# Group 0's x kept in SBUF: the heads' outputs copied straight into the split's input, the fourth heads moved by small DMAs, and the rows of w1 and w2 reordered to match

## The chip, the cores and the metric

One core of a Trainium2 chip runs the whole program. The metric is the time of one execution on the device in microseconds, as the median over several runs. PE is TensorE, DVE VectorE, ACT ScalarE, POOL GpSimd, SP SyncE; SP and POOL also issue DMAs.

## The reference

A gated linear attention, one token after the other, feeds a multiplicative feed-forward block. All inputs are float32 but the four weights, which arrive as 64-bit floats (the kernel reads them as pairs of 32-bit words and makes float32 of them itself).

```python
q, k, v, alpha: (4, 8, 768, 48)            # batch, heads, tokens, head size
for t in range(S):
    state = alpha[:, :, t, :, None] * state + einsum('bhd,bhe->bhde', k[:, :, t], v[:, :, t])
    y[:, :, t] = einsum('bhd,bhde->bhe', q[:, :, t], state)
x = y.transpose(0, 2, 1, 3).reshape(3072, 384)
a = x @ w1                                  # w1, w2: (384, 1024)
b = x @ w2
out = ((a * b) @ w3) @ w_out                # w3: (1024, 1024), w_out: (1024, 384)
```

## The kernel before

The 3072 tokens are 24 chunks of 128 (N), six to a batch entry; one turn n of the main loop, a step, handles one chunk. Three chunks make a group g of 384 tokens (TG), eight groups in all. Part 1 is the attention loop; while it runs, gate work for the groups 0 to 4 is mixed in. Part 2 does the rest of the gates, folds w3 with w_out into one matrix, and multiplies.

A step n of part 1 consists of: `load_a`, `load_kq`, `load_v` (loads for later steps, on SP); `scores(n)` (PE makes k times q into PSUM, VectorE masks it into `ms`, line 457); `transposed(n + 1)` (PE turns `qk` of the next chunk, line 381, ScalarE copies it to `qkT`, line 383); `attend(n - 1)` (PE, line 485, then ScalarE copies the heads' outputs to x, line 489); `outer(n)` (the state's update, lines 393 to 403); `decayed(n + 2)` (VectorE multiplies the loaded k and q by the decays, `qk`, line 359); `logs` and `decays` (the decays `e` of later chunks).

The weights' conversion stands between these: `load_gates` fetches 128 rows and 512 columns of w1 or w2 in one DMA (`raw`, line 236), ScalarE and VectorE make float32 of them (lines 244 to 253) and split it into a high part, a low part `l` (line 262) and a third part. The thirds of the first half are made by PE in `third` (lines 276, 277) and copied by ScalarE (line 278). Six of these conversions have to be done by the end of step 5.

x goes through DRAM: `attend` puts two stores per step into `later`, `store` issues them on SP (line 305) to `xd`, `load_x` brings a group back as `xT` with the model dimension on partitions (line 501), and `split_x` makes three parts of it (ScalarE line 507, VectorE lines 508 and 509). The row order of xT is that of the model dimension, so row p of part kk of the weights is row 128 kk + p of w1 or w2.

`gate` is a generator; `run(pieces)` advances it. A piece is nine matmuls of 128x128 by 128x384 (line 515), for one 128-column tile of w1 or w2: six for the first two parts, then three for the third. The group-0 split stands in step 6 (FIRST), `run(2)` in step 7 and further pieces by a table of step numbers:

```python
pieces = ((3, 3, 2, 0) if n > FIRST + 3 else (0, 3, 3, 0))[(n - FIRST) % 4] if n >= FIRST else 0
```

The order on each engine is not the program's order. A tile framework places the instructions on their engines by its own schedule and by the buffers' dependences; `after_marks` holds an instruction behind a named one in that schedule. Each engine then works through its list in order. SP's DMAs are told apart by eight DMA semaphores, taken in turn.

Of the kernel before, what the change touches and what calls it, by code (L numbers as in the profile page):

```python
# [48 lines left out]
def kernel(  # L49
# [29 lines left out]
    LATE = 10  # L79
    PAIRED = 8  # L80
    TURNED = 8
    assert D <= DP and DM % C == 0 and DF % CW == 0 and S % C == 0 and N % G == 0
    assert DM <= 512 and TG <= 512

# [138 lines left out]
    for x in Ts + decs:  # L223
        nc.gpsimd.memset(x, 0.0)

    def to_fp32(*srcs, width=None):

        n = width or sum(src.shape[1] for src in srcs)
        raw = rawp.tile([C, n], I64, tag="raw", name="raw")
        for i, src in enumerate(srcs):  # L230
            if width:
                rows = ds(i * src.shape[0], src.shape[0])
                to = raw[rows] if len(src.shape) == 2 else raw[rows].rearrange("p (b c) -> p b c", b=src.shape[1])
            else:
                to = raw[:, ds(i * src.shape[1], src.shape[1])]
            nc.sync.dma_start(out=to, in_=src)
        yield
        words = raw.bitcast(U32).rearrange("p (n w) -> p n w", w=2)
        low, high = words[:, :, 0], words[:, :, 1]

        mant = cvt.tile([C, n], FP32, tag="mant", name="mant")
        top = mant.bitcast(U32)
        rest = cvt.tile([C, n], FP32, tag="rest", name="rest", bufs=2)
        nc.scalar.activation(rest, low, AF.Copy, scale=2.0 ** -52)  # L244
        nc.vector.tensor_scalar(top, high, 0x000FFFFF, 0x00100000, op0=ALU.bitwise_and, op1=ALU.bitwise_or)

        power = cvt.tile([C, n], U32, tag="power", name="power", bufs=2)
        nc.vector.tensor_scalar(power, high, 20, 0x7FF, op0=ALU.logical_shift_right, op1=ALU.bitwise_and)  # L248
        nc.scalar.activation(power, power, AF.Relu, scale=2.0 ** 23, bias=rebias)  # L249
        yield  # L250
        nc.vector.scalar_tensor_tensor(mant, top, 2.0 ** -20, rest, op0=ALU.mult, op1=ALU.add)  # L251
        nc.vector.scalar_tensor_tensor(power, high, 0x80000000, power, op0=ALU.bitwise_and, op1=ALU.bitwise_or)  # L252
        nc.vector.tensor_mul(mant, mant, power.bitcast(FP32))  # L253
        yield
        return mant

    def load_gates(i, kk, half):
        w = yield from to_fp32((moe_w1, moe_w2)[i][ds(kk * C, C), ds(half * CW, CW)])
        h, l, m = (w12[half][:, x, i, kk, :] for x in range(3))
        nc.scalar.activation(h, w, AF.Copy, scale=(1.0 - 2.0 ** -13) / P)  # L260
        yield
        mark["l"] = nc.vector.scalar_tensor_tensor(l, h.bitcast(FP32), -P, w, op0=ALU.mult, op1=ALU.add).ins
        done.append((i, kk, half))
        if half:
            nc.vector.scalar_tensor_tensor(m, h.bitcast(FP32), P + 1.0, w, op0=ALU.mult, op1=ALU.subtract)
        else:
            thirds.append((m, h, l))
# [33 lines left out]
    def store():  # L301

        while later:
            dst, src = later.popleft()
            nc.sync.dma_start(out=dst, in_=src)
# [171 lines left out]
    def attend(n):  # L477
        (y, heads), ms, vc = st.pop(("y", n)), st.pop(("ms", n)), st.pop(("v", n))
        for j, i, to in heads:
            if turned(n):  # L480
                w = vts[n % 2][:, j, :] if i else vc[:, 2 * j, :]
                nc.tensor.matmul(to[:, DP:], w, ms[:, i, j, DP:], start=False,  # L482
                                 stop=(j % HP == HP - 1), skip_group_check=True)
            else:
                nc.tensor.matmul(to, vc[:, 2 * j + i, :], ms[:, i, j, :], start=(n % NCH == 0 and j % HP == 0),  # L485
                                 stop=(j % HP == HP - 1), skip_group_check=True)
        x = work.tile([C, HP, 2, C], FP32, tag="x", name="x", bufs=4)
        for i in range(2):
            copied = nc.scalar.copy(x[:, :, i], y[i])
        ends_of_part1[1] = copied.ins  # L490
        x = x.rearrange("p j i t -> p (j i) t")

        g, c = divmod(n, G)
        to = xd[g].rearrange("(b h d) t -> b d h t", b=2, d=D)
        for half in range(2):
            later.append((to[half, :, :, ds(c * C, C)], x[ds(DP * half, D)]))


    def load_x(g, queue=nc.sync):
        st["xT", g] = xp.tile([C, KM, TG], FP32, tag="xT", name="xT")  # L500
        queue.dma_start(out=st["xT", g], in_=xd[g].rearrange("(k p) t -> p k t", p=C))

    def split_x(g, i):
        x = st.pop(("xT", g))
# [79 lines left out]
    def gate(g, f):  # L584
        yield from (late_gate if late else early_gate)(g, f)
# [103 lines left out]
    for n in range(N + 1):  # L689
        if not 1 < n < FIRST:  # L690
            store()
        if n in loads:
            load_x(loads[n])
        if n != 1 and not 2 < n <= FIRST:
            load_a(n + 5)
        raws = (3, 3, 3, 3, 2, 2, 3, 3)[n] if n < 8 else 4
        for m in (n + 3,) * (n <= FIRST) + (n + 4,) * (n >= FIRST):
            load_kq(m)
            if 2 < n <= FIRST and m == n + 3:
                load_a(n + 5)  # L700
            if 1 < n < FIRST:
                store()
            if n < FIRST - 2:
                fetch(raws)
        if n >= FIRST:
            load_v(n + 2)
        if n:
            attend_state(n - 1)
        if n < N:
            scores(n)  # L710
        else:
            for j in range(NP):
                for i in range(2):
                    attend_low(n - 1, j % 2, i, i ^ (j < 2))
        transposed(n + 1)
        if n == 1:
            decays(3)
            load_a(6)
            with after_marks(("e", 3)):
                logs(4)  # L720
        if n == FIRST + 1:
            run(2)
        if n < FIRST:
            with after_marks("pool"):
                load_v(n + 2)
        if n - 2 in begin and n > FIRST:
            g, tiles = begin[n - 2]
            with after_marks(("ms", n), ("qkT", n + 1)):
                split_x(g, 0)
            fill.extend(gate(g, f) for f in tiles)  # L730
        if n == FIRST:
            with after_marks("l", ("qkT", n + 1)):
                split_x(0, 0)
            fill.extend(gate(0, f) for f in begin[n - 3][1])
        pieces = ((3, 3, 2, 0) if n > FIRST + 3 else (0, 3, 3, 0))[(n - FIRST) % 4] if n >= FIRST else 0
        if n == 0:
            with after_marks(("qkT", 0)):
                logs(2)
            decays(2)
            with after_marks(("e", 2)):  # L740
                logs(3)
        early, ready = n < FIRST, len(thirds) if n > 2 else n // 2
        marks = (*[("qkT", n + 1)] * (n < N - 1), *[("qk", n + 1), ("ms", n)] * early, *["x3"] * (n - 2 in begin and n > FIRST))
        if n < N - 2 and n != FIRST:
            with after_marks(*marks):
                convert(2 if early else 1, raws)
        advance(n)
        turn_v(n)
        if n:
            attend(n - 1)  # L750
        outer(n)
        if n > FIRST:
            third(ready)
        run(pieces > 0)
        if early:
            with after_marks(*marks):
                convert(1, raws)
        with after_marks(*[("ms", n)] * (n < 3)):
            decayed(n + 2)
        if not early:  # L760
            with after_marks(*[("qkT", n + 1)] * (n < N - 4)):
                logs(n + 4)
        if n == 4:
            load_x(0)
        convert(early and n > 0, raws)
        run(pieces > 1)
        if n:
            decays(n + 3)
        if n <= FIRST:
            third(ready)  # L770
        if 0 < n < FIRST:
            with after_marks(("e", n + 3)):
                logs(n + 4)
        if n == FIRST:
            with after_marks("x3", ("e", n + 3)):
                convert(2, raws)
        elif n < N - 2:
            convert(n == FIRST - 1 if early else n % 3 == 0, raws)
        if n == FIRST - 1:
            assert len(done) == 2 * KM  # L780
        run(pieces > 2)
        if n == N - 3:
            while begun:
                convert(1)
            weights.extend(load_out(j) for j in range(KF))
            fetch(4)
# [90 lines left out]
```

## Time and profile before

| what | value |
|---|---|
| time, median of 3 runs | 464.25 us (463.48, 464.25, 465.31) |
| span of the profiled execution | 462.8 us; its own total time isn't given beside it |
| busy share of PE, DVE, ACT, POOL | 97%, 80%, 60%, 21% |
| granted clock of TensorE | full in all 40 slices (digit 9) and 1.00 in the stretches |
| line 515, all gate matmuls on x and w | x1152, 337 ns each, 210.2 us |
| chain that ended last | PE 88%, DVE 4%, DMA 4%, ACT 2% |
| DMA packets | 148869, 80.37 MB; 97392 of them under 512 B |
| x stores on SP (`xd<-x`) | x48 of 96 KB, 3.9 us from issue to landing |
| x loads on SP and POOL (`xT<-xd`) | x5 and x9 of 576 KB, 5.0 and 4.7 us |
| weight loads on SP (`raw<-in_moe_w_dram`) | x12 of 512 KB, 5.8 us |

How to read it: a busy share is a mean over stages that have different limits. A chain of waits goes back from the last instruction and names at each point what released the next one. A busy PE has matmul ends that are modelled. Stretches are windows in microseconds from the span's start.

### The profile page before, as it was taken

What the parts mean: (1) busy time and instruction counts of PE and PEld (TensorE: products, weight loads), DVE (VectorE), ACT (ScalarE), POOL (GpSimd) and SP (SyncE); (2) the same over time, 40 slices, a digit from 0 to 9 for tenths busy, and PEclk for the clock granted to TensorE, in tenths of its full rate; (3) what the DMA queues carried; (4) which work ended last, traced back from release to release, by engine and by line L of the source; (5) the groups of instructions that cost most, each with busy time, mean ns of one, the idle gap of its engine ahead of it and who ended that gap; (6) DMA issues with size and microseconds to landing.
All of it is one profiled execution on the core that took longest, in us unless ns stands there. A gap on an engine that the chain in (4) does not pass through costs nothing.

```text
span 462.8 us, 11150 instructions
## 1 busy us (share of the span) xinstructions
PE 446.9 (97%) x4296; PEld 423.2 (91%) x4296; DVE 371.7 (80%) x610; ACT 276.4 (60%) x544; POOL 95.1 (21%) x186
## 2 busy tenths in 40 slices
PE   4998999999999999999999999999999999999996
PEld 2675699898999989999999999999999999999996
DVE  2779997999979988999998999997542967776671
ACT  4685975767658563988875676764545443333430
POOL 6234232325414430121221201212010000000000
PEclk9999999999999999999999999999999999999999
DMA  9999999999999974466856446412115875665511
GB/s 173 254 208 228 261 224 192 248 209 219 184 227 193 234 165 138 130 224 212 235 178 196 146 128 177 149 52 86 51 48 153 243 210 180 186 178 159 166 51 52
DMA packets 148869, 80.37 MB, mean 174 GB/s; under 512 B 97392, under 2 KB 138608, under 8 KB 148816
## 3 DMA queue, kind: packets, MB, share of 16 engines
q1 hardware_dynamic: 143040, 64.44, 57.3%
q0 software_dynamic: 5776, 15.22, 11.0%
q8 instruction: 34, 0.56, 0.5%
q14 instruction: 19, 0.16, 0.1%
HBM read 57.58 MB, written 22.06 MB: 172 GB/s over the span
## 4 chain that ended last, share of the span: by engine, by line
PE 88%; DVE 4%; DMA 4%; ACT 2%; issue 1%; SPq 0%; DVEq 0%; ACTq 0%
PE bank L515 72%; DMA kq<-in_q_dram 3%; PE bank L381 3%; PE bank L430 3%; PE bank L482 2%; PE bank L474 2%; PE bank L340 1%; PE bank L393 1%; PE bank L346 1%; PE bank L454 1%; PE bank L343 1%; PE bank L419 1%; DVE qk L359 1%; DVE ms L457 1%; PE bank L485 1%
## 5 line engine op out<-in xcount | busy, mean ns | idle before, releaser
L515 PE MATMUL bank<-x,w 128*128 128x384 f32 x1152 | 210.2, 337 | 1.7 <-ACT qkT L383 1.1
L515 PEld LDWEIGHTS bank<-x,w 128*128 128x128 f32 x1152 | 200.2, 188 | 4.1 <-ACT qkT L383 1.4
L515 PE MATMUL bank<-w3o,ab 128*128 128x384 f32 x576 | 100.2, 336 | 0.0
L515 PEld LDWEIGHTS bank<-w3o,ab 128*128 128x128 f32 x576 | 99.9, 188 | 0.0
L540 ACT ACTIVATE bank<-bank 128x384 f32<-128x384 f32 x96 | 45.6, 476 | 43.4 <-PE bank L515 43.1
L524 ACT ACTIVATE t<-bank 128x384 f32<-128x384 f32 x64 | 31.9, 499 | 54.9 <-PE bank L515 54.9
L590 POOL DMA_DIRECT2D abd<-ab x45 | 25.8, 573 | 137.9 <-DVE ab L576 121.3
L383 ACT COPY qkT<-bank 128x512 f32<-128x512 f32 x48 | 26.2, 596 | 24.8 <-PE bank L381 24.8
L641 DVE TENSOR_TENSOR ab<-abl,ab 128x1024 fp32r<-128x1024 f32 x24 | 29.3, 1223 | 12.3 <-ACT ab L640 12.3
L640 ACT ACTIVATE ab<-abl 128x1024 fp32r<-128x1024 f32 x24 | 25.5, 1061 | 20.2 <-PE bank L515 18.4
L515 PE MATMUL bank<-wo,w3T 128*128 128x384 f32 x192 | 35.9, 334 | 0.0
L576 DVE TENSOR_TENSOR ab<-bank,r 128x384 f32<-128x384 f32 x44 | 24.1, 548 | 12.5 <-PE bank L515 6.3
L515 PEld LDWEIGHTS bank<-wo,w3T 128*128 128x128 f32 x192 | 33.5, 188 | 0.0
L249 ACT ACTIVATE power<-power,rebias 128x512 uint32<-128x512 uint32 (+1 forms) x36 | 25.3, 701 | 12.6 <-DVE power L248 12.4
L359 DVE TENSOR_TENSOR qk<-kq,e 128x768 f32<-128x768 f32 x24 | 23.1, 964 | 11.3 <-ACT e L350 7.9
L526 DVE SCALAR_TENSOR_TENSOR o<-bank,t 128x384 f32<-128x384 f32 x24 | 13.4, 557 | 23.0 <-issue 13.7
L642 DVE SCALAR_TENSOR_TENSOR ab<-ab,abl 128x1024 fp32r<-128x1024 f32 x24 | 29.2, 1217 | 0.0
L526 DVE SCALAR_TENSOR_TENSOR r<-bank,t 128x384 f32<-128x384 f32 x40 | 22.0, 550 | 6.8 <-PE bank L515 3.4
L251 DVE SCALAR_TENSOR_TENSOR mant<-mant,rest 128x512 f32<-128x512 uint32 (+1 forms) x36 | 23.4, 649 | 3.7 <-ACT rest L244 3.7
L252 DVE SCALAR_TENSOR_TENSOR power<-raw,power 128x512 uint32<-128x512 uint32 (+1 forms) x36 | 23.5, 653 | 2.4 <-ACT power L249 2.4
L253 DVE TENSOR_TENSOR mant<-mant,power 128x512 f32<-128x512 f32 (+1 forms) x36 | 23.6, 655 | 0.5
L244 ACT ACTIVATE rest<-raw 128x512 f32<-128x512 uint32 (+1 forms) x36 | 23.3, 649 | 0.0
(102 smaller groups left out, 675.2 us busy)
## 6 DMA issues: line engine op xcount, KB each, us to landing
abl<-abd SPq DMA_DIRECT2D x24, 512.0 KB, 4.7
abd<-ab POOLq DMA_DIRECT2D x45, 192.0 KB, 3.2
raw<-in_moe_w_dram SPq DMA_DIRECT2D x64, 128.0 KB, 3.4
raw<-in_moe_w_dram SPq DMA_DIRECT2D x12, 512.0 KB, 5.8
xT<-xd POOLq DMA_DIRECT2D x9, 576.0 KB, 4.7
kq<-in_k_dram SPq DMA_DIRECT2D x24, 192.0 KB, 5.2
kq<-in_q_dram SPq DMA_DIRECT2D x24, 192.0 KB, 5.4
xd<-x SPq DMA_DIRECT2D x48, 96.0 KB, 3.9
```

The costliest lines, as they stand in the source:

```text
L249: nc.scalar.activation(power, power, AF.Relu, scale=2.0 ** 23, bias=rebias)
L359: mark["qk", n] = nc.vector.tensor_mul(qks[n % 3][:, :, :, 0:D], st.pop(("kq", n)), st.pop(("e", n)).rearrange("p i (h d) -> p i h d", h=H ...
L383: mark["qkT", n] = nc.scalar.copy(qkT[:, :, :, ds(DP * half, DP)], tp[half]).ins
L515: nc.tensor.matmul(p, w[part][i], x[part][i], start=start and part == parts[0] and i == 0, stop=stop and part == parts[-1] and i == n - 1, ...
L524: nc.scalar.activation(t, p1, AF.Copy, scale=(1.0 + 1.0 / P) * scale)
L526: nc.vector.scalar_tensor_tensor(to, p2, scale, t, op0=ALU.mult, op1=ALU.add)
L540: nc.scalar.activation(p, p, AF.Copy, scale=1.0 + 1.0 / P)
L576: nc.vector.tensor_mul(ab, p, r[0])
L590: (nc.gpsimd if late else nc.sync).dma_start(out=abd[g][:, f, :], in_=ab)
L640: nc.scalar.activation(t[:, 0], ab, AF.Copy, scale=1.0 - 2.0 ** -13)
L641: nc.vector.tensor_sub(t[:, 1], ab, t[:, 0].bitcast(FP32))
L642: nc.vector.scalar_tensor_tensor(t[:, 2], t[:, 0].bitcast(FP32), -1.0 - 1.0 / P, ab, op0=ALU.mult, op1=ALU.add)
```

## The change

For the chunks 0 to 2 (group 0), `attend` no longer stores x to DRAM. ScalarE copies the first three pairs of heads of each half from PSUM straight to their places in `xT`, and the fourth heads into a piece of `x`. Six DMAs per step, of 16 partitions by 128 columns each (8 KB), move those into partitions 48 to 63 and 112 to 127 of `xT`. So a row of xT is no longer a row of x in order: for part kk, partitions 0 to 47 hold head kk, the next 16 hold a third of head 3, and likewise for the second half. `load_gates` fetches the rows of w1 and w2 in that order, with four DMAs instead of one (48, 16, 48 and 16 rows), and `load_x` of the groups 1 to 7 fetches x with four DMAs as well. Group 0 is needed again in part 2: its xT is stored whole to `xd[0]` in step 7, and loaded with one DMA. The split of group 0 moves from step 6 to the end of step 5, its first two pieces of gates from the start of step 7 into step 6, and the thirds of step 6 ahead of them.

```diff
+    def runs(kk):
+        return [(i * DM // 2 + start, size, i * DP + at) for i in range(2)
+                for start, size, at in ((D * kk, D, 0), (D * KM + SD * kk, SD, D))]
...
     def load_gates(i, kk, half):
-        w = yield from to_fp32((moe_w1, moe_w2)[i][ds(kk * C, C), ds(half * CW, CW)])
+        src = (moe_w1, moe_w2)[i][:, ds(half * CW, CW)]
+        w = yield from to_fp32(*(src[ds(start, size)] for start, size, _ in runs(kk)), width=CW, at=[at for *_, at in runs(kk)])
...
         x = work.tile([C, HP, 2, C], FP32, tag="x", name="x", bufs=4)
+        if n < G:
+            if n == 0:
+                st["xT", 0] = xp.tile([C, KM, TG], FP32, tag="xT", name="xT")
+            to, part = st["xT", 0][:, :, ds(n * C, C)], x[:, HP - 1, 1]
+            nc.scalar.copy(part, y[1][:, HP - 1])
+            nc.scalar.copy(to[:, 0::2], y[0])
+            nc.scalar.copy(to[:, 1], y[1][:, 0])
+            for half in range(2):
+                for kk in range(KM):
+                    later.append((to[ds(half * DP + D, SD), kk], part[ds(half * DP + kk * SD, SD)]))
+            return
...
     def load_x(g, queue=nc.sync):
         st["xT", g] = xp.tile([C, KM, TG], FP32, tag="xT", name="xT")
-        queue.dma_start(out=st["xT", g], in_=xd[g].rearrange("(k p) t -> p k t", p=C))
+        if g == 0:
+            queue.dma_start(out=st["xT", g], in_=xd[g].rearrange("(p k) t -> p k t", k=KM))
+            return
+        for at in range(0, C, DP):
+            h = xd[g][ds(at // DP * DM // 2, DM // 2)]
+            queue.dma_start(out=st["xT", g][ds(at, D)], in_=h[0:KM * D].rearrange("(k p) t -> p k t", p=D))
+            queue.dma_start(out=st["xT", g][ds(at + D, SD)], in_=h[KM * D:].rearrange("(k p) t -> p k t", p=SD))
...
+        if n == FIRST + 1:
+            nc.sync.dma_start(out=xd[0].rearrange("(p k) t -> p k t", k=KM), in_=x0)
...
-        if n == FIRST + 1:
-            run(2)
...
-        if n == FIRST:
-            with after_marks("l", ("qkT", n + 1)):
-                split_x(0, 0)
-            fill.extend(gate(0, f) for f in begin[n - 3][1])
-        pieces = ((3, 3, 2, 0) if n > FIRST + 3 else (0, 3, 3, 0))[(n - FIRST) % 4] if n >= FIRST else 0
+        pieces = ((3, 3, 2, 0) if n > FIRST + 3 else (2, 3, 3, 0))[(n - FIRST) % 4] if n >= FIRST else 0
...
-        if n > FIRST:
+        if n >= FIRST:
             third(ready)
...
-        if n == 4:
-            load_x(0)
...
-        if n <= FIRST:
+        if n < FIRST:
             third(ready)
...
         if n == FIRST:
-            with after_marks("x3", ("e", n + 3)):
+            with after_marks(("e", n + 3)):
                 convert(2, raws)
...
         if n == FIRST - 1:
             assert len(done) == 2 * KM
+            x0 = st["xT", 0]
+            with after_marks("l"):
+                split_x(0, 0)
+            fill.extend(gate(0, f) for f in begin[FIRST - 3][1])
```

More of the change, by code (lines that the diff above doesn't have):

```diff
@@ L81 @@
     TURNED = 8
+    SD = D // KM
+    assert H == 2 * (KM + 1) and D % KM == 0 and D + SD == DP
     assert D <= DP and DM % C == 0 and DF % CW == 0 and S % C == 0 and N % G == 0
@@ L224, with to_fp32 @@
         nc.gpsimd.memset(x, 0.0)
-    def to_fp32(*srcs, width=None):
+    def runs(kk):
+        return [(i * DM // 2 + start, size, i * DP + at) for i in range(2)
+                for start, size, at in ((D * kk, D, 0), (D * KM + SD * kk, SD, D))]
+    def to_fp32(*srcs, width=None, at=None):
         n = width or sum(src.shape[1] for src in srcs)
@@ L231, in to_fp32 @@
             if width:
-                rows = ds(i * src.shape[0], src.shape[0])
+                rows = ds(at[i] if at else i * src.shape[0], src.shape[0])
                 to = raw[rows] if len(src.shape) == 2 else raw[rows].rearrange("p (b c) -> p b c", b=src.shape[1])
```

## The prediction

> **What bounds the kernel now.** I read the page's slices first, then busy time by stretches, the chain of waits, the waits of VectorE, the timeline of VectorE and ScalarE around the first split, and the DMA issues. After these I compared the order of instructions of the two kernels, engine by engine.
>
> The slices (40 of 11.6 us each) show three engines full at once in the first third:
>
> ```profile
> PE   4998999999999999999999999999999999999996
> DVE  2779997999979988999998999997542967776671
> DMA  9999999999999974466856446412115875665511
> ```
>
> The stretches say where TensorE still has idle time (columns: stretch, length, then busy us of PE, PEld, DVE, ACT, POOL, and the granted clock, DMA share and GB/s):
>
> ```profile
> 24.40:54.70 30.30, 27.41 (x409) 20.79 (x408) 26.15 (x44) 22.60 (x50) 10.17 (x17) 1.00 1.11 233
> 54.70:57.70 3.00, 3.00 (x38) 2.13 (x37) 2.71 (x5) 3.00 (x8) 0.83 (x2) 1.00 1.07 275
> 57.70:80.00 22.30, 22.30 (x318) 21.00 (x316) 19.76 (x38) 13.99 (x33) 7.14 (x15) 1.00 1.10 210
> 80.00:86.40 6.40, 5.30 (x125) 4.54 (x121) 5.63 (x9) 5.14 (x12) 2.31 (x3) 1.00 0.91 240
> ```
>
> From 54.7 us PE is full, with one hole of 1.1 us near 86, up to the end of part 1 (99.48 of 100.60 us busy from 86.4 to 187). So the end of the kernel is the moment at which PE becomes full, plus the work then left. Before 54.7 PE has 30.30 - 27.41 = 2.9 us of idle time, the most that an earlier start of gates can fill. The chain of waits shows who hands over to PE:
>
> ```profile
> 27.01 7.37 DMA kq<-in_q_dram
> 34.51 0.96 DVE qk L359
> ...
> 53.93 0.91 PE bank L343 x2
> ...
> 56.16 1.09 PE bank L454 x16
> 57.26 0.49 PE bank L381 x16
> 57.75 3.35 PE bank L515 x18
> ```
>
> VectorE leads, with one long wait for a load, until 50.4; then PE. Three pieces of attention work, 0.91 + 1.09 + 0.49 = 2.49 us (the decays of step 9, the scores of step 7, the transposes of step 8), stand on PE just ahead of the first 18 gate matmuls. Meanwhile VectorE and ScalarE make the split:
>
> ```profile
> 53.50 0.69 DVE L262 SCALAR_TENSOR_TENSOR w<-w,mant 128x512 fp32r<-128x512 f32 x1
> 54.11 1.28 DVE L457 TENSOR_TENSOR ms<-bank,keep 128x512 int32<-128x512 int32 x2
> 55.94 1.36 DVE L508 TENSOR_TENSOR x<-xT,x 128x1152 fp32r<-128x1152 f32 x1 [0.28 <-ACT x L507]
> 53.74 1.10 ACT L383 COPY qkT<-bank 128x512 f32<-128x512 f32 x2
> 54.68 1.22 ACT L507 ACTIVATE x<-xT 128x1152 fp32r<-128x1152 f32 x1
> ```
>
> The last weight part (L262) ends at 54.19 and the split starts on ScalarE at 54.68: x waited for neither its stores nor its load. xT had long landed, since L501 was issued at 49.08. So the trip through DRAM that the change takes away isn't what ends last here.
>
> **The change, part by part.** The profiled execution has a span of 462.8 us; the median of the runs is 464.25, 1.45 above. I work out a shift and add it to the median. A measurement of this kernel tells about 0.5% (2.3 us) from no change.
>
> *x of group 0 stays in SBUF.* Gone are six stores (0.44 us of SP each, median) and one load of 576 KB. New are 18 moves of 8 KB and, in step 7, a 576 KB store of xT. DMA work up to step 6 falls, by about 3 x 0.5 us for the stores (two that follow each other land 0.2 us apart) and about 2 us for the load. The path isn't there, so I take nothing; at best it shortens the waits for kq. The store in step 7 falls into DMA queues that are full (share 1.10), but qk finds its kq landed from 57.7 to 80, so: nothing. If that cover went, one such load (5.0 us to landing) would be its price.
>
> *ScalarE's copies.* Two copies of 256 columns (0.36 us each) become one of 256 and two of 128. From 384 columns at 0.48 and 256 at 0.36 a copy of 128 is about 0.24: +0.12 us in each of three steps, ScalarE being idle 25% of that stretch. Nothing; 0.4 us without the cover.
>
> *Weights.* Each of 12 loads of 512 KB becomes four (192, 64, 192, 64 KB), and xT loads of groups 1 to 7 four as well: SP gets 36 + 12 + 12 + 1 - 1 = 60 more issues, POOL 24 more. On POOL a load is issued right after the split before its own, a whole visit of gates ahead; one issue there is some 0.57 us (the row of `abd`), and PE is full: nothing, and 1.7 us per load without that cover. On SP, the order shows that each issue from the ninth on waits for one of eight DMA semaphores in turn, so at most eight transfers are under way. A step of the early part has some 13 issues instead of 6 or 7. At 0.5 us each they need 6.5 us of a step of about 7, and behind them stand the kq loads. I take nothing for the likeliest case, since qk is placed one place later in the new order (next), and keep the other end as a rival. [...]
>
> *VectorE's order.* In the new order qk of step 8 comes after the split and no longer ahead of it: -0.95 us. Each qk from 4 on stands one place later against the weight conversion, so its waits go: 2.36 and 0.22 for kq, 0.66 for ScalarE, 0.28 before L508, together 3.5 us. But ms of a step now follows close behind the qk that feeds it, and between them lies transposes 0.72, copies 1.07, scores 1.16, with hand-overs 3.1 us. Ms of step 6 has only L262 (0.69) in between: a stall of 2.4. Ms of step 5 has 2.36 us of work: 0.7. The split waits on ScalarE behind the qkT copies of step 7: transposes 0.72, copies 1.07, split 1.22 with hand-overs 3.2, less L262 and T (1.04): 2.1. New stalls 5.2. L508 would start at 55.94 - 0.95 - 3.5 + 5.2 = 56.7, 0.75 us later. The stalls may be half as long where PE answers sooner (-2.6), and nothing may be won from the old waits (+3.5): -1.9 to +4.3.
>
> *PE's order.* The 18 gate matmuls now stand ahead of the 2.49 us of decays, scores and transposes. These filled the time in which the split was made; now PE has only the thirds there (1.3 us), waits for L508, and does the 2.49 us afterwards. Sum: 0.75 + 2.49 = 3.2 us. No later row gives it back: PE has only 1.1 us idle from 57.7 to 86.4. There, split of group 1 stands on ScalarE one pair of qkT copies later than now. By the rows those 18 matmuls, which end at 88.76, would end near 90.6 (transposes until 82.98, copies 1.1, x copies 0.65, split 1.18, L508 1.36, 3.35 of PE): +1.9. Against this, PE's delay of 3.2 gives ScalarE and VectorE time to be ready, down to -1.1. I take 0 and keep both ends.
>
> So the forecast is 464.25 + 3.2 = 467.5.
>
> **The rivals.**
> - *Faster.* The freed DMA time brings kq sooner, the stalls behind qk are short, and the gates fill PE's early holes: up to 2.9 us, 461.4. For: DMA share 1.11 and the 2.36 us wait. Against: VectorE does 26.15 of those 30.30 us, and the split isn't made by a DMA. It decides if L508 starts before about 53.4, since 2.49 us more stand behind the gates. 14%.
> - *No change.* L508 starts near 53.5 to 55, or PE's later holes swallow the shift: 464.3. 20%.
> - *Eight in flight.* 13 issues per step at 3.9 to 5.3 us of latency, eight at a time, need 6.3 to 8.6 us against about 7.0 now. Over three steps that is about nothing to 4.8; with 4.5 to 5.3 us the middle is 2.9. kq and raw then come late in steps 4 to 6 and VectorE waits: 467.5 + 2.9 = 470.4. For: SP issues without a pause up to 57 us. Against: kq is needed one place later. 16%.
> - That the change doesn't do what it says I hold as excluded: the order shows the gates before the scores of step 7.
>
> **How the numbers follow.** Forecast 50%, faster 14%, no change 20%, eight in flight 16%. The forecast's own range is 465.2 to 470; about a quarter of it lies within 2.3 us of 464.25. So faster 0.14; same 0.20 + 0.12 = 0.32; slower 0.38 + 0.16 = 0.54. The range goes from 461.5 (most of the first rival is left out) to 471.5.
>
> **What would show it.** Right: L508's first run starts at or after 56 us; PE idles between the thirds and the first 18 gate matmuls; VectorE waits at ms for the scores of steps 5 and 6; qk no longer waits 2.4 us for kq. For eight in flight: qk or the weights' first VectorE step waiting for DMA by over 1 us in steps 4 to 6. Wrong: the gates begin before 55.5 us, or part 1 ends (last x store, 185.6 us now) no later than now. Then the order view overstates stalls that the chip doesn't have.

## The result, and the profile after

The changed kernel takes 510.14 us (median of 6 runs, 507.65 to 513.19) where the kernel before takes 464.53 us (6 runs). The ratio is 1.098, with a 95% interval of 1.095 to 1.102: 45.6 us slower. The direction was forecast, the size was not: 467.5 us, with 471.5 us as the upper end.

The profiled execution took 512.61 us, of which 510.9 us are its span. In this kernel's line numbers qk is L367, transposes L389, scores L462, masks ms L465, weight parts L252 to L270, split L532 to L534, gates L540, and stores and moves on SyncE L313. The slices of the page after:

```profile
PE   4868669969978997999999999999999999999997
DVE  2547646859784796797899989999973387777771
PEclk9869858998978998999999999999999999999999
DMA  9998859997895879653668755454211685555511
```

TensorE and VectorE both have holes in the first half. TensorE's granted clock, at digit 9 in all 40 slices before, is under it in nine of the first sixteen, and at 5 in the lowest. No engine has taken over. The same stretches as before (stretch, length, busy us of PE, PEld, DVE, ACT, POOL, granted clock, DMA share, GB/s):

```profile
24.40:54.70 30.30, 24.07 (x288) 18.29 (x285) 17.11 (x29) 16.55 (x38) 9.23 (x14) 0.78 0.96 153
54.70:57.70 3.00, 3.00 (x33) 1.93 (x33) 0.00 (x0) 1.35 (x3) 0.46 (x1) 0.86 1.35 162
57.70:80.00 22.30, 14.06 (x130) 10.89 (x129) 12.01 (x20) 11.25 (x22) 5.02 (x9) 0.62 0.67 132
80.00:86.40 6.40, 5.61 (x52) 4.43 (x50) 5.20 (x8) 3.25 (x7) 0.23 (x1) 1.00 1.12 202
```

VectorE does 17.11 us of work in the first stretch where it did 26.15, and the DMAs bring 153 GB/s instead of 233. From 57.7 to 80 us, where TensorE had been full, it is busy for 14.06 of 22.30 us, and that at a mean clock of 0.62. VectorE's timeline shows the pattern of the loss (start, length, what, and in brackets the idle time before it and what ended that):

```profile
50.53 0.95 DVE L367 TENSOR_TENSOR qk<-kq,e 128x768 f32<-128x768 f32 x1
...
58.17 1.29 DVE L465 TENSOR_TENSOR ms<-bank,keep 128x512 int32<-128x512 int32 x2 [4.27 <-PE bank L462]
...
62.25 0.95 DVE L367 TENSOR_TENSOR qk<-kq,e 128x768 f32<-128x768 f32 x1
63.12 0.69 DVE L270 SCALAR_TENSOR_TENSOR w<-w,mant 128x512 fp32r<-128x512 f32 x1
69.99 1.29 DVE L465 TENSOR_TENSOR ms<-bank,keep 128x512 int32<-128x512 int32 x2 [6.19 <-PE bank L462]
...
79.26 1.36 DVE L533 TENSOR_TENSOR x<-xT,x 128x1152 fp32r<-128x1152 f32 x1 [0.80 <-ACT x L532]
```

And TensorE's, in between:

```profile
56.98 1.16 PE L462 MATMUL bank<-qkT 48*128 48x128 f32 x16
58.07 1.09 PE L493 MATMUL bank<-ms,v 128*64 128x128 f32 x16
63.35 1.11 PE L389 MATMUL bank<-ident,qk 64*128 64x64 f32 x16 [4.18 <-DVE qk L367]
...
67.88 2.08 PE L462 MATMUL bank<-qkT 48*128 48x128 f32 x16
```

The two engines wait for each other by turns. TensorE stands until VectorE has made qk at 62.25; VectorE then has one short piece (L270) and stands until the scores that come from that qk are there. A step takes 11.8 us (58.17 to 69.99), where before it took some 6 (from the qk at 28.7 us to that at 52.5 there are four). After the pause TensorE's granted clock is 0.50 (63.3 to 70.0 us), and the next scores take 2.08 us against 1.16. Over the whole span the two engines' waits for each other, and two waits for ScalarE that stand beside them, are (us in total, times, longest):

```profile
DVE ms L465 <- PE bank L462: 17.6, 4, 6.6
PE bank L389 <- DVE qk L367: 13.5, 5, 4.2
DVE mant L258 <- ACT rest L251: 10.7, 7, 3.1
PE bank L348 <- ACT x L324: 4.3, 1, 4.3
```

Not all of the 17.6 us belong to this loop. The longest wait, 6.6 us, ends at 36.13 us. The scores for that mask stood on TensorE behind the four matmuls of the decays (L348), and these had waited 4.3 us for ScalarE's logarithms (L324). The two waits in the timeline above, 4.27 and 6.19 us, are those between a qk and the scores made from it.

The first split starts on VectorE at 79.26 us instead of 55.94, 23 us late; the second at 113.8 instead of 81.2, the sixth at 245.9 instead of 190.0. So about half of the loss is there before the first gate runs, and the rest comes until the sixth split (8 us of it are regained later, among the gates). By TensorE's account the span's 48.1 us more are 467.8 - 446.9 = 20.9 us of busy time, for the same 4296 instructions, and 27.2 us of idle time. By its groups they lie mostly in the attention's short matmuls and hardly in the gates (L540 on x and w: 211.8 us, 210.2 before).

### The profile page after: what moved, and what is told of

Its sections match the earlier page's. It is cut to its first block, busy times and chain, and to the rows that moved or that the text cites. A ratio compares the mean times of both kernels' runs of the same rounds, so it can differ in the third digit from the quotient of the medians.

```text
span 510.9 us, 11326 instructions
## 1 busy us (share of the span) xinstructions
PE 467.8 (92%) x4296; PEld 438.5 (86%) x4296; DVE 372.9 (73%) x610; ACT 280.9 (55%) x547; POOL 106.7 (21%) x210
## 4 chain that ended last, share of the span: by engine, by line
PE 75%; DMA 6%; DVE 5%; ACT 3%; issue 2%; SPq 1%; POOL 1%; POOLq 0%; ACTq 0%; DVEq 0%
PE bank L540 63%; PE bank L389 2%; PE bank L438 2%; DMA ends<-e 2%; DMA dec<-ends 2%; PE bank L490 2%; PE bank L482 1%; ACT x L532 1%; DMA ac<-in_alpha_dram 1%; PE bank L493 1%; PE bank L348 1%; PE bank L427 1%; PE bank L462 1%; PE bank L401 1%; DVE x L534 1%
## 5 line engine op out<-in xcount | busy, mean ns | idle before, releaser
L540 PE MATMUL bank<-x,w 128*128 128x384 f32 x1152 | 211.8, 339 | 4.1 <-ACT x L532 1.7
L540 PEld LDWEIGHTS bank<-x,w 128*128 128x128 f32 x1152 | 201.5, 189 | 6.9 <-ACT x L532 1.8
L540 PE MATMUL bank<-w3o,ab 128*128 128x384 f32 x576 | 100.2, 336 | 0.0
L540 PEld LDWEIGHTS bank<-w3o,ab 128*128 128x128 f32 x576 | 99.9, 188 | 0.0
L540 PE MATMUL bank<-wo,w3T 128*128 128x384 f32 x192 | 35.9, 334 | 0.0
L540 PEld LDWEIGHTS bank<-wo,w3T 128*128 128x128 f32 x192 | 33.5, 188 | 0.0
L389 PE MATMUL bank<-ident,qk 64*128 64x64 f32 x384 | 20.2, 257 | 13.7 <-DVE qk L367 13.5
L389 PEld LDWEIGHTS bank<-ident,qk 64*128 64x128 f32 x384 | 16.9, 164 | 17.4 <-issue 12.7
L258 DVE SCALAR_TENSOR_TENSOR mant<-mant,rest 128x512 f32<-128x512 uint32 (+1 forms) x36 | 23.6, 654 | 10.8 <-ACT rest L251 10.7
L256 ACT ACTIVATE power<-power,rebias 128x512 uint32<-128x512 uint32 (+1 forms) x36 | 25.1, 698 | 10.3 <-DVE power L255 10.3
L367 DVE TENSOR_TENSOR qk<-kq,e 128x768 f32<-128x768 f32 x24 | 22.8, 951 | 8.5 <-ACT e L358 8.5
```

Of the source, the lines that this page charges most:

```text
L389: nc.tensor.transpose(tp[half][:, i, j, :], qk[s, i, 2 * j:2 * j + 2, :], ident[s, s])
L540: nc.tensor.matmul(p, w[part][i], x[part][i], start=start and part == parts[0] and i == 0, stop=stop and part == parts[-1] and i == n - 1, ...
```

## The experiments

Three theories stood at first. **O**: the order of the engines' instructions, which the framework fixes when the program is built, costs the time, and it changed because of edits elsewhere. **D**: the added DMAs cost it when they run. **S**: the copies, the moves and the earlier split cost it. To tell O from D, the order of one build was imposed on another: each instruction of an engine was tied to the one ahead of it in the wanted order, by an edge that orders the queue and adds no wait. This is what "pinned" means below:

```python
order = [ins[at + k] for at, n in runs for k in range(n)]      # ins: the engine's instructions as traced
for a, b in zip(order, order[1:]):
    tc.add_manual_dep(b, a.name, mybir.DependencyInfo(mybir.DependencyClass.NoSync, mybir.DependencyReason.DATA), reason="pinned")
```

The median of the kernel before lay between 464.2 and 465.3 us in the comparisons; ratios are to it, with 95% intervals.

### Order against DMAs

**Four-part weight loads in the kernel before.**

```diff
-        w = yield from to_fp32((moe_w1, moe_w2)[i][ds(kk * C, C), ds(half * CW, CW)])
+        src = (moe_w1, moe_w2)[i][ds(kk * C, C), ds(half * CW, CW)]
+        w = yield from to_fp32(*(src[ds(a, s)] for a, s in ((0, 48), (48, 16), (64, 48), (112, 16))), width=CW, at=(0, 48, 64, 112))
```

> The kernel before with one edit: each of its twelve weight loads of part 1 is issued as four DMAs of 48, 16, 48 and 16 partitions that bring the same rows to the same places; x goes by DRAM as before. When the program is built, this alone turns VectorE's order in steps 1 to 6 into that of the changed kernel (the products qk of step n+2 stand behind the masks ms of step n and behind a conversion, instead of ahead of ms). Theory O (the loss is the order of the engines' instructions): most of the loss comes already here, 490 to 510 us. Theory D (the loss is what the added DMAs themselves do when they run: 36 more issues on SyncE at 0.42 us or somewhat more each, about 15 us if all of it were on the path, and queueing): 470 to 482 us. Theory S (the loss is in the copies, the moves and the earlier split): 464 us, no change.

Measured: 492.9 us, ratio 1.058 (1.053 to 1.064). Twelve loads cut in four cost 28 us.

**The same, with the order of before** (`pinned` for VectorE, ScalarE, TensorE).

> The same four DMAs per weight load as in the run before it, but the order of VectorE, ScalarE and TensorE is pinned, instruction by instruction, to that of the kernel before (edges that order an engine's queue and add no wait). Theory O: the loss is gone, 463 to 468 us. Theory D: the DMAs run all the same, so it stays where the unpinned one is (470 to 482 us by its own sizes). Theory S: 464 us.

Measured: 477.4 us, 1.026 (1.021 to 1.031). The order is worth about 15 us of the 28; the DMAs alone cost 12.8 us. Neither theory has it all. What the DMAs do is in the waits of VectorE in this run:

```profile
DVE qk L347 <- DMA kq<-in_q_dram: 12.4, 3, 5.3
```

The same row of before had 2.6 us. The third load of kq was issued at 10.3 us, against 9.0, and the eighth at 50.6, against 39.3.

**The order of after in the kernel before** (`pinned` for VectorE and TensorE; no added DMA).

> The kernel before with all its own DMAs (one for each load, x by DRAM), and VectorE and TensorE pinned to the order that the changed kernel's program has when its first split and gates are left in their old steps; ScalarE is left free. Theory O: the loss comes without any of the added DMAs, 490 to 512 us. Theory D: 464 to 466 us. Theory S: 464 us.

Measured: 493.7 us, 1.060 (1.055 to 1.065). Without any added DMA, the order costs 29 us. Only VectorE and TensorE were held to it; ScalarE, SyncE and GpSimd were left free. SyncE's issues come in the order of before up to 55 us and in another from there on, so the 29 us are those of the two engines' order with what followed from it. Waits between 24 and 70 us in this run:

```profile
DVE ms L444 <- PE bank L441: 10.1, 4, 5.3
PE bank L368 <- DVE qk L346: 10.4, 4, 4.4
```

Both stand by turns as in the changed kernel, though all loads are those of before. In the kernel before the first was 0.5 us and the second not there.

**The changed kernel with the order of before** (`pinned` for three engines).

> The changed kernel complete, with all of its DMAs, copies, moves and its earlier split, and with VectorE, ScalarE and TensorE pinned to the order that the program has when each load is one DMA (which is the order of the kernel before except for the first split and the first gates, a step sooner). Theory O: 459 to 467 us, near the forecast of 467.5 or better. Theory D: 505 to 512 us, as the changed kernel. Theory S: 505 to 512 us as well, as copies, moves and split are all here.

Measured: 484.7 us, 1.042 (1.038 to 1.046). The order is 510.1 - 484.7 = 25.4 us of the change's loss, and 20.0 us stay with the right order.

### What the 20 us are

**Striped weight loads:** as many DMAs, each to every fourth partition.

```diff
+        w = yield from to_fp32(*(src[r::4] for r in range(4)), width=CW, step=4)      # to = raw[i::4]
```

> As the pinned kernel with four DMAs per weight load (477.4 us), with as many DMAs, as many packets of 4096 bytes and the same pinned order, but each of the four takes every fourth partition (32 of them, spread over all 128) instead of a run of 48 or 16 neighbours. In the profiles so far a packet of 4096 bytes before 80 us took 0.161 us (median) where a load was one DMA over 128 partitions and 0.289 us where it was runs of 48 and 16. Theory P (DMAs into few neighbouring partitions are slow by the packet, whatever their number): the packets are back near 0.16 to 0.20 us and the time at 464 to 469 us. Theory N (the number of DMAs costs: their issue on SyncE and their fixed work on the queues): 475 to 479 us.

Measured: 474.9 us, 1.024 (1.018 to 1.030). The packets of 4096 bytes are back at a median of 0.161 us, and the first split at 59.0 us instead of 65.6, as P has it. But 7 us more were lost until the fourth split, so the total says N.

**Single loads in the changed kernel** (weights and later x in one DMA each; moves and copies stay).

> The changed kernel with one DMA for each weight load and for each later load of xT, as before, so that the rows of the weights and of x stand in other places than the copies put them (the products are of other rows than the reference's). Copies into xT, the eighteen moves and the earlier split and gates stay, and the order comes out as that of the kernel before but for the split. If the split loads are the whole loss: 460 to 467 us. If the moves and copies cost too (theory M, 18 more DMAs of 8 KB among the loads of steps 3 to 6): 470 to 476 us.

Measured: 475.5 us, 1.025 (1.022 to 1.027). Theory M: without any split load the rest of the change costs 11 us.

**Single loads of x alone, weights in four** (pinned).

> The pinned changed kernel (484.7 us) with one DMA for each later load of xT instead of four (its rows then stand in other places than the weights' rows, so other products are taken), the weights still in four; the same pinned order. If the four-part xT loads cost in part 1 (the second split came 15.5 us later than before there, the first 8.3): 476 to 480 us. If not: 483 to 486 us.

Measured: 482.6 us, 1.038 (1.035 to 1.042), beside 1.042 (1.038 to 1.046) with four. At most a small part; the intervals overlap.

**The split, gates and thirds in their old steps** (pinned).

> The changed kernel with all its DMAs and copies, but its first split, first gates and thirds back in the steps that the kernel before has them in, pinned to that order. Against the pinned changed kernel (484.7 us) this is the earlier split alone. Theory S (the earlier split stands in the way of masks and products that wait for late loads): 478 to 483 us. If the earlier split brings the 3 us that a faster first group could bring: 486 to 489 us. If it does nothing: 484 to 485 us.

Measured: 483.5 us, 1.042 (1.038 to 1.045), as with the earlier split. Theory S falls, and so does the hope that the earlier split brings anything here.

**36 tiny DMAs in the kernel before** (pinned).

```diff
+        for to, src in more:                  # three per weight load: 16 partitions, 16 bytes each, to a spare tile
+            nc.sync.dma_start(out=to, in_=src)
```

> The kernel before, its weight loads whole, with three further DMAs on SyncE behind each of the twelve weight loads, each of which brings 16 bytes to each of 16 partitions of a spare tile that nothing reads; order of VectorE, ScalarE and TensorE pinned to that of before. 36 DMAs more, as with the four-part loads, but next to no bytes and none in the loads' way. Theory Q (what costs is the number of DMAs in SyncE's queue, which issues one after the other): 471 to 477 us, like the striped loads (474.9 us). If only bytes and packets count: 464 to 467 us.

Measured: 468.8 us, 1.008 (1.005 to 1.011), under what Q expected and over "nothing". The number of DMAs by itself costs about 4 us, not 10.

**Six moves instead of eighteen** in the changed kernel (pinned).

```diff
-                    later.append((to[ds(half * DP + D, SD), kk], part[ds(half * DP + kk * SD, SD)]))
+            if n == G - 1:                    # part: one tile for all three steps
+                        later.append((st["xT", 0][ds(half * DP + D, SD), kk], st["part"][ds(half * DP + kk * SD, SD)]))
```

> The pinned changed kernel (484.7 us) with the fourth heads' 48 rows of all three steps gathered in one tile and moved once, by six DMAs of 24 KB in step 5, instead of eighteen of 8 KB in steps 3 to 5. Same bytes, twelve DMAs less on SyncE in the crowded steps. Theory Q: 477 to 481 us. If the moves cost by their bytes or by their place ahead of the split alone: 484 to 486 us.

Measured: 480.4 us, 1.033 (1.028 to 1.038): 4 us back.

**Six moves and single loads** (pinned).

> The changed kernel with single loads (475.5 us; rows of weights and of x in other places, so other products are taken) and the six moves instead of eighteen, pinned to the order that it had. SyncE then has no more DMAs up to the split than in the kernel before. Theory Q: the loss is gone but for what lies in the copies and the earlier split, 463 to 468 us. If copies, split or the moves' wait cost by themselves: 472 to 476 us.

Measured: 465.6 us, 1.003 (1.000 to 1.006). Of the 11 us of the run with single loads and eighteen moves, 10.0 are gone. Between 24 and 100 us VectorE waited 5.4 us for kq there, and here no such wait is listed. Copies, six moves and the earlier split together cost about 1 us and bring nothing: the first split starts at 52.46 us, 3.5 us earlier than in the kernel before, but the third no earlier than there (110.9 against 111.0). The first stretches look like those of before:

```profile
24.40:54.70 30.30, 28.38 (x416) 21.54 (x408) 26.83 (x45) 24.94 (x56) 10.89 (x18) 1.00 1.02 210
...
57.70:80.00 22.30, 22.30 (x361) 20.50 (x363) 18.71 (x38) 14.05 (x31) 7.74 (x15) 1.00 1.04 225
```

Why eighteen moves are dear can be read from SyncE's timeline of the pinned changed kernel (start, length of the whole group); no run tests this time alone:

```profile
32.70 7.81 SPq L300 DMA_DIRECT2D xT<-x  x6
...
47.44 4.18 SPq L300 DMA_DIRECT2D xT<-x  x6
...
56.08 4.83 SPq L300 DMA_DIRECT2D xT<-x  x6
61.01 0.53 SPq L142 DMA_DIRECT2D kq<-in_k_dram  x1
```

The three groups hold SyncE for 16.8 us of 28, and the next kq stands behind each. 6.5 of the 16.8 us are waits for ScalarE, the rest is issue. In the kernel before, the two stores in their place held it for 3.33, 1.16 and 1.17 us, and 2.6 us of the 3.33 were a wait for ScalarE. The six moves of 24 KB in the run with single loads hold it for 4.9 us, as long as six of 8 KB.

### What else was in the order

The striped run, and that with single loads, left GpSimd's order free. It had changed there, and TensorE waited a little for GpSimd's copies of v. **G** was that this is where their second loss came from. In the run with six moves GpSimd's order was free too and stood nearly as before, so its 10.0 us are those of the moves with GpSimd's order.

**GpSimd's order of the striped run in the kernel before**, nothing else.

> The kernel before with all its own DMAs and its own order on VectorE, ScalarE and TensorE; only GpSimd's part 1 is pinned to the order that it had in the striped run, where it was left free (there the copies vt of v and the decays' DMAs stand in other places). Theory G (the 7 us that the striped run lost between 84 and 150 us, with TensorE waiting for vt, are GpSimd's order): 468 to 472 us. Theory Q (that loss, too, came from DMAs): 464 to 466 us.

Measured: 465.5 us, 1.001 (0.998 to 1.003). G falls for the striped run's order. That of the run with single loads is close to it and wasn't tried.

**Four-part loads in runs, all four engines pinned to before.**

> The kernel before with its weight loads as four DMAs of 48, 16, 48 and 16 partitions, and now all four engines, GpSimd's part 1 too, in the order of before, instruction by instruction; only SyncE differs. Pinned without GpSimd it took 477.4 us. Theory G: 470 to 474 us, and the first split as late as there (65.6 us). Without an effect of GpSimd's order: 476 to 479 us.

Measured: 478.5 us, 1.028 (1.023 to 1.032), as without GpSimd.

**Striped loads, all four engines pinned.**

> The same, all four engines in the order of before, with the striped loads (every fourth partition). Pinned without GpSimd they took 474.9 us, with the first split at 59.0 us against 65.6 us. Theory G with theory P (packets into few neighbouring partitions are slow): 465 to 469 us, some 5 us under the loads in runs of 48 and 16. If the place of the partitions doesn't matter: as the loads in runs.

Measured: 473.6 us, 1.018 (1.013 to 1.023). The total is over the expectation, the gap of 4.9 us to the loads in runs is as P has it. Among packets that started before 58 us, those of 4096 bytes had a median of 0.267 us in runs, 0.166 striped, 0.160 in the kernel before.

**The changed kernel, all four engines pinned.**

> The changed kernel complete, with VectorE, ScalarE, TensorE and GpSimd's part 1 pinned to the order of the run with single loads and six moves (465.6 us). Pinned without GpSimd it took 484.7 us. Theory G: 477 to 481 us. If GpSimd's order adds nothing here: 483 to 486 us.

Measured: 488.2 us, 1.051 (1.044 to 1.058): nothing comes back with GpSimd's order.

**qk behind the masks, one step of lead left**, in the kernel before.

```diff
-        with after_marks(*[("ms", n)] * (n < 3)):
+        with after_marks(*[("ms", n)] * (n < 8)):
             decayed(n + 2)
```

> The kernel before with one more order mark: in steps 3 to 7 the product qk of step n+2 is queued on VectorE behind the masks ms of step n (in the kernel before it stands ahead of them from step 3 on). Nothing else of VectorE's order moves but the pieces beside it. Theory O1 (the place of qk is what the order costs): most of the 29 us that the order of after cost with the DMAs of before, 480 to 495 us. Theory O2 (the loss of that order is spread over conversions, masks and scan sums, and qk alone is a step's wait here and there): 465 to 472 us.

Measured: 465.7 us, 1.001 (0.998 to 1.004). Theory O1 falls: one place later costs nothing, as long as a step of lead stays.

**No lead:** qk of step n + 1 behind the masks of step n.

```diff
+        if 3 < n < 9:
+            with after_marks(("ms", n)):
+                decayed(n + 1)
         transposed(n + 1)
```

> The kernel before with the product qk of step n+1 queued behind the masks ms of step n, for steps 4 to 8, that is one step later than in the run that left one step of lead and cost nothing: between qk of a step and the masks of the same step VectorE now has only one conversion. Theory L (the order costs when qk has no step of lead: TensorE then waits for qk, and VectorE waits at ms for the scores of the same step, by turns): both waits appear, 1 to 2 us each in each of five steps, the first split at 60 to 66 us and the time at 469 to 478 us. If the order's 29 us are the conversions' places or the later steps': 464 to 467 us.

Measured: 479.0 us, 1.028 (1.024 to 1.032), a little over the expected range. The waits of TensorE between 24 and 100 us:

```profile
PE bank L381 <- DVE qk L359: 13.0, 5, 6.6
```

The loss came a step later than expected: the first split at 59.0 us, the second at 96.7 instead of 81.2. The waits at ms stayed small (1.7 us), since a conversion still stands between. The schedule also moved some of ScalarE's and SyncE's instructions, so the 13.7 us are those of the missing lead with what followed from it.

**The lead given back to the changed kernel**, in steps 3 to 7.

> The changed kernel as it is, with one thing in its order changed: in steps 3 to 7 the product qk of step n+2 is put ahead of the masks ms of step n on VectorE, as in the kernel before. All DMAs and the rest of its order stay. Theory L: 6 to 14 us of the loss come back, 496 to 504 us, and the waits at ms (17.6 us) shrink. If the lead of qk is not what the order costs: 507 to 512 us.

Measured: 506.9 us, 1.091 (1.084 to 1.097): 3 us back, less than expected. Up to the first split the lead did what theory L says: the waits at ms between 24 and 70 us fall from 17.1 to 5.4 us, and the split starts at 68.3 instead of 79.3 us. VectorE now waits for late kq instead:

```profile
DVE qk L367 <- DMA kq<-in_q_dram: 5.9, 3, 4.1
```

Of these 11 us, 6 are left at the sixth split (239.5 against 245.9 us) and at the end of the two profiled executions (spans of 504.6 and 510.9 us), and 3 in the medians. The rest is lost again behind the first split.

## Why the prediction was wrong

**What bounds the kernel, and the trip through DRAM.** Right about x, which was not what ended last: the run with single loads and six moves has the whole gain of the change and is 1.4 us from the kernel before. Its first split starts at 52.46 us, earlier than the sign set for the faster rival (53.4), and still that rival's 461.4 us was not reached. "Had long landed" was too strong, though: loads of xT took 4.2 us or more from issue to landing, so this one landed 1.4 us ahead of the split at the earliest.

The premise that the end is "the moment at which PE becomes full, plus the work then left" failed. It needs TensorE to stay full from the first gates on. From 86.4 to 187 us TensorE was busy for 88.70 of 100.60 us in the changed kernel (99.48 before). So 23 us of delay at the first split became 56 at the sixth, and with the lead given back, 11 us there became 6 at the sixth (239.5 against 245.9 us).

**VectorE's order.** The mechanism was right and named: ms close behind the qk that feeds it, and the chain of transposes, copies and scores in between. The size failed. I summed new stalls of 2.4, 0.7 and 2.1 us (ms of step 6, ms of step 5, the split), from pieces with the durations of the profile before. Measured were 6.2, 4.3 and 2.5 us, 13.0 instead of 5.2. What the sum had not at all is the 6.6 us at an earlier ms and the waits of VectorE's conversions for ScalarE (L258). The loop closes in both directions: TensorE waits for qk while VectorE waits for scores, and each wait moves the other. The forecast's 3.2 us for both orders stand against 25.4 us (changed kernel, order taken away) and 29.0 us (order alone, put into the kernel before). Only a part of these lies ahead of the first split, which came 12 us late with the order alone. From there to the sixth split another 20 us were added, in steps that the sum did not cover, beyond the split of group 1.

**Engine durations.** I used rows at a granted clock of 1.00 for a state in which TensorE pauses. Sixteen score matmuls of the same shape took 2.08 us after a pause, at a granted clock of 0.50, and 1.16 us at 1.00 (56.98 to 58.20 us).

**Weights.** "I take nothing" was wrong by 12.8 us. The chain of before spoke against it. The prediction shows one load of kq on it, 7.37 us from 27.01, and speaks of "one long wait for a load". A second one stands a step later:

```profile
39.74 7.11 DMA kq<-in_q_dram
```

What makes kq late thus had a way to the end. The rival of eight in flight priced it at 2.9 us and pointed to the right sign: qk waiting for kq, 12.4 us with the order held. My reason for taking nothing, that qk stands a place later in the new order, was no cover. In the changed kernel qk has no long wait for kq, as I wrote, but the order that saves it costs more, and with the old order the late kq are waited for. SyncE was not the whole of it either: 36 tiny DMAs cost about 4 us, and of the remaining 9 us about 5 go with where the parts lie and how they are cut (478.5 us in runs, 473.6 striped).

**x of group 0 stays in SBUF.** "I take nothing" was wrong by 10.0 us for twelve of the eighteen moves where each load is one DMA, and by 4.3 us beside the four-part loads. I counted their bytes (8 KB) against the stores that went away, and not SyncE's time: 16.8 us for the eighteen.

**PE's order, ScalarE's copies, the earlier split.** Copies, split and six moves together: 1.4 us. The 2.49 us behind the gates show in the run with six moves: its first split is 3.5 us earlier than that of before, its second group of gates (61.20 against 62.51 us) only 1.3, with the decays, scores and transposes in between, as forecast.

**What would show it.** L508's successor started after 56 us (79.26), VectorE waited at ms in steps 5 and 6, and in the changed kernel qk has no long wait for kq: as written, and compatible with a loss ten times the size. One sign did not come: TensorE did not idle between the thirds and the first gates, which follow without a gap at 79.7 us. It idled ahead of the transposes, 4.1 us for the qk of step 7, and 0.3 and 0.5 us inside the 18 gate matmuls. That the direction came out as forecast owes little to the sum: its largest term, the 2.49 us on TensorE, belongs to what cost 1.4 us in all. Added up, the sum's own ends run from 463.7 to 472.9 us, wider than the stated range and still far from 510.

The terms do not add up: 12.8 (weights), 10.0 (moves), 2 (x loads) and 1.4 are 26 us against the 20.0 of the pinned kernel. Part of that is that moves and four-part loads delay the same kq (qk waits 12.4 us for kq with the four-part loads alone, 12.6 with the moves as well, both pinned): beside four-part loads, twelve moves fewer bring 4.3 us and not 10.0.

**Open.** Striped loads cost 8 to 10 us, with packets about as fast as before (0.166 us against 0.160), where as many tiny DMAs cost 4; no run tells what makes the rest. Which places of the order between the first and the sixth split cost the 20 us wasn't tried either, nor how much of them is the order of SyncE and ScalarE, which were free in that run. No version here is faster than the kernel before, so none is put forward.

## What to carry to other kernels

Where a framework places the instructions by a schedule of its own, an edit to a load can be an edit to the order: cutting twelve DMAs in four turned VectorE's queue round, and pinning the old order gave 15 of 28 us back. Read the new order for the lead between a producer and the engine that answers it; one step of lead was free here (ratio 1.001), and no lead cost 14 us with what followed from it (1.028). In a stage where SyncE issues without a pause, price every added DMA by its time on that queue and by who stands behind it, not by its bytes alone: eighteen moves of 8 KB held SyncE for 16.8 us. Follow the stages behind the first delay as well: 23 us late at the first split were 56 at the sixth.

## What the runs showed of the hardware

- A load of the same rows in runs of 48 and 16 neighbouring partitions moved its 4096-byte packets in 0.267 us, striped over all partitions in 0.166 us, and as one DMA, in the kernel before, in 0.160 us (medians of the packets that started before 58 us; the first two with all four engines pinned). No run separates the place of the partitions from the sizes of the parts (192 and 64 KB against 128).
- TensorE's granted clock was 0.62 in a stretch in which it was busy 63% of the time (57.7 to 80 us), and 1.00 there before. Behind a pause of 4.2 us it was 0.50 (63.3 to 70.0 us), and score matmuls of the same shape took 2.08 instead of 1.16 us. Over the whole span the mean was 0.949 with 467.8 us of busy time, and 1.00 with 446.9 us before; no run tells how much of the 20.9 us between them is the clock's.
- Moves inside SBUF of 8 KB held SyncE for 0.7 to 1.3 us each, as means of six (16.8 us for eighteen, of which 6.5 us are waits for ScalarE); moves of 24 KB held it for 0.8 us each. Joined threefold they cost 10.0 us less with single loads (465.55 against 475.53 us), and 4.3 us less beside four-part loads (480.4 against 484.7 us).
